# Adding the memory sums' epsilon during eviction, with new cuts around the weighing and a new order of banks in the tail

## The chip, the cores and the metric

The kernel runs on one core of one Trainium2 chip. The metric is device microseconds (us) of a whole execution. Most executions of one kernel agree within 0.3%. A profiled execution is one execution; its span is from first to last instruction. All comparisons below are between runs in the fast state (granted TensorE clock 1.0).

## The reference, cut to what matters

The program computes `x + A(layernorm(x)) + B(x)`. B is a gated-MLP-like block over the sequence and is not touched. A is attention in four segments of 512 rows with 32 heads, plus a linear "memory" that is carried from segment to segment:

```python
for s in range(N):                                   # 4 segments
    logits = einsum('bhqd,bhkd->bhqk', qs, ks) * scale + mask
    p = softmax(logits); a_dot = einsum('bhqk,bhkd->bhqd', p, vs)
    pq  = phi(qs)
    num = einsum('bhld,bhde->bhle', pq, M)
    den = einsum('bhld,bhd->bhl', pq, z)[..., None] + 1e-06      # the epsilon in question
    a_mem = num / den
    outs.append(g * a_mem + (1.0 - g) * a_dot)
    M, z = M + ..., z + ...
return o @ wo
```

Of the kernel before, what the change touches and what calls it, by code (L numbers as in the profile page):

```python
# [7 lines left out]
ALU = mybir.AluOpType  # L8
# [378 lines left out]
class _Kernel:  # L387
# [33 lines left out]
    def alloc(self):  # L421
        k = _Walk(self.mem, 0, self.G_AT)

        def one(name, shape, dtype):
            t, (r,) = k.take(name, shape, dtype)
            setattr(self, name, t)
            setattr(self, "R_" + name, r)

        one("ident", [P, P], BF16)
        self.brow1, self.R_brow1 = k.take("brow1", [P, 32], BF16, 5)  # L430
        self.brow2, self.R_brow2 = k.take("brow2", [P, 32], BF16, 5)
        one("bcol", [P, 2, 32], BF16)
        one("b1c", [P, N_FCH], F32)
        one("b2c", [P, N_TCH], F32)
        one("beta", [P, N_HEAD], BF16)
        one("gcol", [P, N_HEAD], F32)
        one("gate", [P, N_GRP, 2, 4], F32)
        one("eps8", [P, 2, 4], F32)
        self.ln_st, self.R_st = k.take("ln_st", [P, N_TCH, 12], F32, N_TCH)
        self.ln_mv = k.take("ln_mv", [P, N_TCH, 2], F32)[0]  # L440
        self.ln_rs, self.R_rs = k.take("ln_rs", [P, N_TCH, 2], F32, N_TCH)
        self.R_rs0 = Res("rs0")
        one("expo", [P, N_TCH], F32)
        self.ln_sm = k.take("ln_sm", [P, N_TCH, 1], F32)[0]
        self.srec, self.R_srec = k.take("srec", [P, 2, 32], F32, 2)
        self.R_out = [Res(f"out{c}") for c in range(N_TCH)]

        e = _Walk(self.mem, self.G_AT, self.B_AT)
        one_e = e.take("junk", [P, D_MODEL], BF16)
        self.junk, (self.R_junk,) = one_e  # L450
        self.warm, (self.R_warm,) = e.take("warm", [P, 512], BF16)
        e.at = self.G_AT + 14336
        self.w1early, self.R_w1e = e.take("w1early", [P, N_TCH, 512], BF16, N_TCH)
        e.at = self.G_AT + 3 * 14336
        self.xin, self.R_xin = e.take("xin", [P, N_TCH, D_MODEL], BF16, N_TCH)

        b = _Walk(self.mem, self.B_AT + 6400, self.SB_END - self.SB_BASE)
        self.h = [[None, None], [None, None]]
        R = [[None, None], [None, None]]
        for k2 in range(2):  # L460
            both, res = b.take(f"h{k2}", [P, 2, 8, 512], F16, 1)
            self.mem.live.pop()
            for d in range(2):
                self.h[k2][d] = both[:, d]
                R[k2][d] = [Res(f"h{k2}{d}_{i}") for i in range(8)]
                lo = self.SB_BASE + b.at - 16384 + 8192 * d
                self.mem.live.append((lo, lo + 8192, R[k2][d]))
            setattr(self, f"h_{k2}", both)
        self.R_h = R
        self.hT, self.R_hT = [], []  # L470
        for i in (0, 1, 3):
            t, (r,) = b.take(f"hT{i}", [P, 8, 512], F16)
            self.hT.append(t[:])
            self.R_hT.append([r])
        self.hT.insert(2, self.h[0][1])
        self.R_hT.insert(2, R[0][1])
        self.w1s, self.R_w1s = [], []
        for i in range(2):
            t, (r,) = b.take(f"w1s{i}", [P, N_TCH, 256], BF16)
            self.w1s.append(t)  # L480
            self.R_w1s.append(r)
        self.s1, self.R_s1 = [], []
        for i in range(2):
            t, r = b.take(f"sum1_{i}", [P, 4, 8, P], F16, 4)
            self.s1.append(t)
            self.R_s1.append(r)
        self.tmp, self.R_tmp = [], []
        for i in range(6):
            t, (r,) = b.take(f"part{i}", [P, 512], F32)
            self.tmp.append(t)  # L490
            self.R_tmp.append(r)
# [55 lines left out]
    def gates(self):  # L547

        fw = self.fw
        fw.op("pool", lambda e: e.memset(self.eps8[:, 0, :], 0.0), writes=[self.R_eps8])  # L550
        fw.op("pool", lambda e: e.memset(self.eps8[:, 1, :], MEM_EPS), reads=[self.R_eps8], writes=[self.R_eps8])
        fw.op("act", lambda e: e.activation(self.gcol[:], self.beta[:], ACT.Exp, scale=-1.0),
              reads=[self.R_beta], writes=[self.R_gcol])
        fw.op("dve", lambda e: e.tensor_scalar(self.gcol[:], self.gcol[:], 1.0, None, op0=ALU.add),
              reads=[self.R_gcol], writes=[self.R_gcol])
        fw.op("dve", lambda e: e.reciprocal(self.gcol[:], self.gcol[:]), reads=[self.R_gcol], writes=[self.R_gcol])
        gv = self.gcol[:].rearrange("p (g r) -> p g r", r=4)
        fw.op("dve", lambda e: e.tensor_scalar(self.gate[:, :, 0, :], gv, -1.0, 1.0, op0=ALU.mult, op1=ALU.add),
              reads=[self.R_gcol], writes=[self.R_gate])
        fw.op("dve", lambda e: e.tensor_copy(self.gate[:, :, 1, :], gv),  # L560
              reads=[self.R_gcol, self.R_gate], writes=[self.R_gate])
# [580 lines left out]
    def before_attention(self, p):  # L1142
# [42 lines left out]
        elif p == 3:  # L1185
            self.pT = take("pT", [P, 2, 4, PT_COLS], BF16)[0]
            base = self.mem.live.pop()
            self.R_pu = [[Res(f"pu{b}{k}", dict(base[2][0].r)) for k in range(4)] for b in range(2)]
            self.R_pd = [[Res(f"pd{b}{k}", dict(base[2][0].r)) for k in range(4)] for b in range(2)]
            self.mem.live.append((base[0], base[1], [r for rows in self.R_pu + self.R_pd for r in rows]))  # L1190
            self.xnT[1], self.R_xnT[1] = take("xnT1", [P, N_DCH, SEG_L], BF16, 4)
            w = _Walk(self.mem, self.B_AT, self.B_AT + self.S2_AT)
            self.MZ32, self.R_MZ32 = w.take("MZ32", [P, N_GRP, GW], F32, N_GRP)
            self.MZbf, self.R_MZbf = w.take("MZbf", [P, N_GRP, GW], BF16, N_GRP)
            self.diag, (self.R_diag,) = w.take("diag", [P, 4, VW], F32)
            self.oT, self.R_oT = [], []
            for k in range(2):
                t, r = w.take(f"oT{k}", [P, N_GRP, SEG_L], BF16, N_GRP)
                self.oT.append(t)
                self.R_oT.append(r)  # L1200
            w = _Walk(self.mem, self.B_AT + 88320, self.B_AT + 96512)
            self.fin, self.R_fin = [], []
            for k in range(4):
                t, r = w.take(f"fin{k}", [P, D_MODEL], BF16, 2)
                self.fin.append(t)
                self.R_fin.append(r)
            fw.op("dve", lambda e: e.memset(self.diag[:], 0.0), writes=[self.R_diag])
            for r in range(4):
                fw.op("dve", lambda e: e.memset(self.diag[32 * r:32 * r + 32, r, :], 1.0),
                      reads=[self.R_diag], writes=[self.R_diag])  # L1210
# [161 lines left out]
    def weigh(self, u, part):  # L1372
# [37 lines left out]
        else:  # L1410
            q0 = (0, 2, 3)[part]
            dst = self.ost[o][:].rearrange("p (q a) x -> p q (a x)", q=4)[:, q0:q0 + n, 0:GW]
            src = self.ps[:, b, 0:n * GW].rearrange("p (q y) -> p q y", y=GW)
        fw.op("dve", lambda e: e.tensor_copy(dst, src), reads=[self.R_bank[b]], writes=[self.R_ost[o][part]])  # L1414
        if upd:
            src = self.ps[:, b, 2 * GW:3 * GW]
            m32, mbf = self.MZ32[:, g, :], self.MZbf[:, g, :]
# [9 lines left out]
    def combine(self, u):  # L1427
# [22 lines left out]
        def scales():  # L1450
            sums = ost[:, :, D_HEAD].rearrange("p (q a) -> p q a", q=4)
            rv = rec.rearrange("p (q a) -> p q a", q=4)
            e8 = self.eps8[:].rearrange("p k r -> p (k r)")[:, None, :].to_broadcast([P, 4, 8])
            g8 = self.gate[:, g, :, :].rearrange("p k r -> p (k r)")[:, None, :].to_broadcast([P, 4, 8])
            fw.op("dve", lambda e: e.tensor_tensor(rv, sums, e8, op=ALU.add), reads=R_ost + [self.R_eps8], writes=[R_rec])
            fw.op("dve", lambda e: e.reciprocal(rec, rec), reads=[R_rec], writes=[R_rec])
            fw.op("dve", lambda e: e.tensor_tensor(rv, rv, g8, op=ALU.mult), reads=[R_rec, self.R_gate], writes=[R_rec])

        def products():
# [58 lines left out]
    def attention(self):  # L1518
# [11 lines left out]
        for u in range(N_UNIT):  # L1530
# [13 lines left out]
            if u in self.XN_AT[::4]:  # L1544
                self.xn_load(xn)
                self.xn_load(xn + 1)
            if u < 10 or u >= 14 and total <= 26:
                cuts = self.cut(total, (0, 4, 2, 4, 1, 13, 8) if even else (7, 3, 2, 4, 1, 15))
            else:
                cuts = self.cut(total, (0, 4, 2, 2, 2, 14, 8) if even else (7, 3, 2, 2, 2, 16))  # L1550
# [46 lines left out]
    def tail(self):  # L1597
# [5 lines left out]
        fw.wait_outputs(3)  # L1603

        def product(n, j0, j1, cols=((0, 512),)):
            i, h, b = n // 2, n % 2, (0, 1, 2, 3, 6, 7, 5, 4)[n]
            for p, (c0, c1) in enumerate(cols):
                with fw.group(reads=self.R_wo[j0:j1] + self.R_oT[s % 3][j0:j1], writes=[self.R_bank[b]]):
                    for jc in range(j0, j1):
# [24 lines left out]
        product(4, 0, 7)  # L1634
        self.o_transpose(u, 4)
        product(3, 6, 7)
        product(5, 0, 7)
        for n in range(6):
            product(n, 7, 8)
        product(6, 0, 8)  # L1640
        product(7, 0, 8, ((0, 256), (256, 384), (384, 512)))

# [27 lines left out]
```

## The kernel before: what the change touches

Attention is cut into 32 units u (4 segments of 8 groups of 4 heads). In unit u, TensorE does the logits of u in steps, and the *weighing* (softmax weights and memory times values) of unit u-1 in three parts; dense 512-column matmuls (the projections `wq`, `wv`, `wo`) fill the gaps. `cuts` says how many of them stand between those steps. Between the logits and the weighing, ScalarE takes the exponential and the pool engine (POOL, GpSimd) masks the diagonal blocks in place.

```python
# --- attention(), unit u: where the dense matmuls stand
if u < 10 or u >= 14 and total <= 26:
    cuts = self.cut(total, (0, 4, 2, 4, 1, 13, 8) if even else (7, 3, 2, 4, 1, 15))
else: ...
self.dense(cuts[0]);  self.logits(u, 0)
self.dense(cuts[1]);  self.weigh(u - 1, 0)
self.dense(cuts[2]);  self.weigh(u - 1, 1)
self.dense(cuts[3]);  self.weigh(u - 1, 2)
#   ... VectorE's work is queued: scales, phi_q(u), products, add (then the transposing DMA oT <- o_s)
self.dense(cuts[4]);  self.logits(u, 1)
if even:
    self.dense(cuts[5]); self.logits(u, 2)      # third logits: blocks of u AND of u + 1
self.dense(rest)
# --- weigh(): a part leaves PSUM (12 x 33 columns = 396, or 264)
fw.op("dve", lambda e: e.tensor_copy(dst, src), reads=[self.R_bank[b]], writes=[self.R_ost[o][part]])
# --- combine(), segments 1 to 3
def scales():
    fw.op("dve", lambda e: e.tensor_tensor(rv, sums, e8, op=ALU.add), ...)      # + epsilon, 128 x 32
    fw.op("dve", lambda e: e.reciprocal(rec, rec), ...)
    fw.op("dve", lambda e: e.tensor_tensor(rv, rv, g8, op=ALU.mult), ...)
def products():   # prod <- ost * srec, 128 x 1024, both inputs in SBUF
def add():        # o_s <- prod + prod
# --- tail(): the last output product, after the last unit
i, h, b = n // 2, n % 2, (0, 1, 2, 3, 6, 7, 5, 4)[n]         # the bank of product n
product(0, 0, 6); product(1, 0, 6); self.weigh(u, 0); self.weigh(u, 1); product(2, 0, 6); self.weigh(u, 2)
for step in self.combine(u): step()
product(3, 0, 6)
for n in range(3): product(n, 6, 7)             # needs unit 30's transposed result (jc = 6)
product(4, 0, 7); self.o_transpose(u, 4); product(3, 6, 7)
product(5, 0, 7)
for n in range(6): product(n, 7, 8)
...
```

An even unit's third logits belong half to the next unit. So the weighing of an odd unit's result happens in an even unit and needs that odd unit's first mask.

## Time and profile before

| | before |
|---|---|
| median of 3 runs | 654.29 us (654.28 to 654.56) |
| median of 6 runs (these 3 and 3 more), beside the kernel after | 654.42 us (654.12 to 654.98) |
| span of the profiled run | 652.2 us |

From the page of the kernel before, the line of busy times (us, share of the span, instructions) and the first line of the chain that ended last:

```profile
PE 646.7 (99%) x4611; PEld 303.1 (46%) x4611; DVE 439.9 (67%) x829; ACT 281.5 (43%) x305; POOL 154.9 (24%) x181
...
PE 90%; DVE 4%; DMA 2%; ACT 1%; POOL 1%; issue 1%; DVEq 0%
```

TensorE is the limit. The Trainium skill ("Perfetto Trace Analysis", § Identifying the Most-Contended Engine) warns that matmul busy time is a poor measure, because matmuls are pipelined; this case agrees, since the page says 98 or 99% for every fast run here, and 99% for the one that saves 3.3 us. What was used instead is the distance between the starts of neighbouring matmuls in the trace, less the length of the matmul (0.213 us for 512 columns) and the fixed step at a change of matmul kind. What remains is called a *stall* below.

Groups of instructions of the kernel before (out<-in, shapes, count | busy us, mean ns | idle before it), VectorE and then POOL:

```profile
L1460 DVE TENSOR_TENSOR prod<-ost,srec 128x1024 bf16<-128x1024 bf16 x24 | 35.1, 1461 | 0.0
L1414 DVE CAST ost<-ps_all 128x396 bf16<-128x396 f32 x48 | 26.4, 564 | 10.6 <-PE ps_all L199 10.2
...
L1455 DVE TENSOR_TENSOR srec<-ost,eps 128x32 f32<-128x32 bf16 x24 | 4.8, 202 | 0.3
...
L1367 POOL TENSOR_SCALAR_AFFINE_SELECT pT<-pT 128x512 bf16<-128x512 bf16 x128 | 106.3, 847 | 160.9 <-ACT pT L1363 160.9
```

The product `prod` and the mask `pT<-pT` have means (1461 and 847 ns) that hide two populations. The timeline of the kernel before shows them (columns: start us, duration us, engine, line, operation). Unit 24 first (VectorE, the pool engine, TensorE), then unit 26 (the same order):

```profile
575.27 0.69 DVE L1229 SCALAR_TENSOR_TENSOR pqT<-qT,mtmp 128x512 bf16<-128x512 bf16 x1
575.88 1.68 DVE L1460 TENSOR_TENSOR prod<-ost,srec 128x1024 bf16<-128x1024 bf16 x1
...
575.84 0.63 POOL L1367 TENSOR_SCALAR_AFFINE_SELECT pT<-pT 128x512 bf16<-128x512 bf16 x1 [2.78 <-ACT pT L1363]
...
576.25 0.82 PE L199 MATMUL ps_all<-wo,oT 128*128 128x512 bf16 x3
576.91 0.26 PE L199 MATMUL ps_all<-vA,pT 128*128 128x33 bf16 x4
...
590.06 1.22 DVE L1460 TENSOR_TENSOR prod<-ost,srec 128x1024 bf16<-128x1024 bf16 x1
...
590.43 1.34 POOL L1367 TENSOR_SCALAR_AFFINE_SELECT pT<-pT 128x512 bf16<-128x512 bf16 x1 [2.55 <-ACT pT L1363]
...
591.92 0.25 PE L199 MATMUL ps_all<-vA,pT 128*128 128x33 bf16 x4 [0.19 <-POOL pT L1367]
```

In unit 24 the mask starts 0.04 us before the product: the mask takes 0.63 us and the product 1.68. In unit 26 the product starts first: the product takes 1.22 us and the mask 1.34. Whoever comes first runs undisturbed (the mask in 0.63, the product in 1.22 us). TensorE's weighing (`vA,pT`) waits for the mask, so the second order is the expensive one: in unit 24 the weighing starts 0.22 us after the start of the 512-column matmul before it, in unit 26 it starts 0.57 us after, so it stalls for 0.35 us.

The tail of the kernel before on TensorE and on the queue of SyncE, which issues the transposing DMA:

```profile
631.74 1.90 PE L199 MATMUL ps_all<-wo,oT 128*128 128x512 bf16 x8
633.89 2.75 PE L199 MATMUL ps_all<-wo,oT 128*128 128x512 bf16 x12 [0.24 <-ACT pT L1363]
...
637.49 1.19 SPq L221 DMA_TRANSPOSE oT<-o_s  x1
```

The first product of the tail waits for the last exponential (bank 0 is still being read). Unit 30's result is issued for its transpose at 637.49 us, and the product that needs it loses 0.16 us.

### The profile page before, as it was taken

What the parts mean: (1) busy time and instruction counts of PE and PEld (TensorE: products, weight loads), DVE (VectorE), ACT (ScalarE), POOL (GpSimd) and SP (SyncE); (2) the same over time, 40 slices, a digit from 0 to 9 for tenths busy, and PEclk for the clock granted to TensorE, in tenths of its full rate; (3) what the DMA queues carried; (4) which work ended last, traced back from release to release, by engine and by line L of the source; (5) the groups of instructions that cost most, each with busy time, mean ns of one, the idle gap of its engine ahead of it and who ended that gap; (6) DMA issues with size and microseconds to landing.
All of it is one profiled execution on the core that took longest, in us unless ns stands there. A gap on an engine that the chain in (4) does not pass through costs nothing.

```text
span 652.2 us, 11204 instructions
## 1 busy us (share of the span) xinstructions
PE 646.7 (99%) x4611; PEld 303.1 (46%) x4611; DVE 439.9 (67%) x829; ACT 281.5 (43%) x305; POOL 154.9 (24%) x181
## 2 busy tenths in 40 slices
PE   9999999999999999999999999999999999999998
PEld 3444444444444444444444444444545444454444
DVE  6975775665655673745637325767898988887895
ACT  7542232232210000111101047778767788888760
POOL 2500000000011220120201203434333445544450
PEclk9999999999999999999999999999999999999999
DMA  8804242242498937629263956979644576355424
GB/s 300 217 0 130 65 116 79 65 124 70 129 265 216 231 96 210 171 87 258 66 193 116 257 136 156 190 182 227 124 120 109 152 164 144 90 115 123 114 81 138
DMA packets 190123, 95.00 MB, mean 146 GB/s; under 512 B 108664, under 2 KB 176248, under 8 KB 190072
## 3 DMA queue, kind: packets, MB, share of 16 engines
q1 hardware_dynamic: 189928, 94.25, 56.9%
q8 instruction: 36, 0.59, 0.4%
q14 instruction: 15, 0.12, 0.1%
q10 hardware_dynamic: 144, 0.03, 0.0%
HBM read 69.23 MB, written 11.53 MB: 124 GB/s over the span
## 4 chain that ended last, share of the span: by engine, by line
PE 90%; DVE 4%; DMA 2%; ACT 1%; POOL 1%; issue 1%; DVEq 0%
PE ps_all L199 90%; ACT pT L1363 1%; DMA w2s<-in_B_w_dram 1%; POOL pT L1367 1%; DVE fin L1617 1%; DVE ln_st L590 1%; DVE sum L651 0%; DVE prod L1460 0%; DMA xin<-in_A_x_dram 0%; DVE h L630 0%; POOL ln_rs L614 0%; DVE mtmp L1229 0%; DVE mtmp L1227 0%; DVE ost L1414 0%; DVE part L692 0%
## 5 line engine op out<-in xcount | busy, mean ns | idle before, releaser
L1363 ACT ACTIVATE pT<-ps_all 128x2048 bf16<-128x2048 f32 x80 | 150.2, 1877 | 47.2 <-PE ps_all L199 46.8
L1367 POOL TENSOR_SCALAR_AFFINE_SELECT pT<-pT 128x512 bf16<-128x512 bf16 x128 | 106.3, 847 | 160.9 <-ACT pT L1363 160.9
L692 DVE TENSOR_TENSOR part<-ps_all,part 128x512 f32<-128x512 f32 x84 | 57.7, 690 | 108.9 <-PE ps_all L199 88.2
L1078 POOL TENSOR_TENSOR part<-part,stg 128x512 f32<-128x512 f32 x24 | 33.0, 1402 | 285.0 <-DVE part L692 268.1
L749 ACT ACTIVATE g<-part,b1c 128x512 f16<-128x512 f32 x36 | 26.0, 722 | 99.0 <-DVE part L692 99.0
L199 PE MATMUL ps_all<-wv,xnT 128*128 128x512 bf16 x256 | 68.2, 380 | 0.2
L199 PE MATMUL ps_all<-xnT,wq 128*128 128x512 bf16 x256 | 65.6, 380 | 0.0
L199 PE MATMUL ps_all<-wo,oT 128*128 128x512 bf16 (+2 forms) x272 | 64.3, 367 | 0.2 <-ACT pT L1363 0.2
L1414 DVE CAST ost<-ps_all 128x396 bf16<-128x396 f32 (+2 forms) x96 | 44.3, 473 | 27.3 <-PE ps_all L199 26.6
L697 ACT ACTIVATE part<-ps_all 128x512 f32<-128x512 f32 x24 | 14.0, 596 | 101.4 <-PE ps_all L199 67.1
L199 PEld LDWEIGHTS ps_all<-vA,pT 128*128 128x128 bf16 x1280 | 45.5, 96 | 21.5 <-DVE ost L1414 3.3
L199 PE MATMUL ps_all<-g,sum 128*128 128x512 f16 x224 | 51.0, 379 | 0.0
L199 PE MATMUL ps_all<-g,w2s 128*128 128x512 f16 x224 | 51.0, 379 | 0.0
L199 PE MATMUL ps_all<-gT,sum 128*128 128x512 f16 x224 | 50.3, 379 | 0.1
L199 PE MATMUL ps_all<-vA,pT 128*128 128x33 bf16 x1280 | 48.5, 178 | 0.7 <-POOL pT L1367 0.6
L199 PE MATMUL ps_all<-h,sum 128*128 128x512 f16 x192 | 45.2, 379 | 0.0
L199 PE MATMUL ps_all<-h,w1s 128*128 128x512 f16 x192 | 44.9, 379 | 0.0
L199 PE MATMUL ps_all<-hT,sum 128*128 128x512 f16 x192 | 43.6, 379 | 0.0
L199 PEld LDWEIGHTS ps_all<-wo,oT 128*128 128x128 bf16 x272 | 23.8, 97 | 27.1 <-issue 4.9
L1460 DVE TENSOR_TENSOR prod<-ost,srec 128x1024 bf16<-128x1024 bf16 x24 | 35.1, 1461 | 0.0
L199 PEld LDWEIGHTS ps_all<-gT,sum 128*128 128x128 f16 x224 | 21.8, 98 | 26.8 <-DVE gT L666 0.6
L199 PEld LDWEIGHTS ps_all<-g,w2s 128*128 128x128 bf16 x224 | 21.9, 98 | 26.4
(118 smaller groups left out, 862.2 us busy)
## 6 DMA issues: line engine op xcount, KB each, us to landing
w2s<-in_B_w_dram SPq DMA_DIRECT2D x8, 1792.0 KB, 9.5
w1s<-in_B_w_dram SPq DMA_DIRECT2D x12, 1024.0 KB, 5.6
wq<-in_A_wq_dram SPq DMA_DIRECT2D x32, 256.0 KB, 3.4
xs<-in_A_x_dram SPq DMA_DIRECT2D x24, 256.0 KB, 3.4
stg<-in_A_x_dram SPq DMA_DIRECT2D x16, 256.0 KB, 2.8
out_dram<-stg SPq DMA_DIRECT2D x16, 256.0 KB, 3.8
wk<-in_A_wk_dram SPq DMA_DIRECT2D x16, 256.0 KB, 3.4
fin<-out_dram SPq DMA_DIRECT2D x16, 256.0 KB, 3.3
```

What stands on the lines that cost most here:

```text
L199: ins = self.nc.tensor.matmul(*args, **kwargs)
L590: fw.op("dve", lambda e: e.bn_stats(st[:, 6 * h:6 * h + 6], src[:, 512 * h:512 * h + 512]), reads=[self.R_xin[c]], writes=[R])
L692: self.fw.op("dve", lambda e: e.tensor_tensor(self.tmp[dst][:], self.bank(b), self.tmp[src][:], op=ALU.add), reads=[self.R_bank[b], self.R ...
L697: self.fw.op("act", lambda e: e.activation(self.tmp[dst][:], self.bank(b), ACT.Copy), reads=[self.R_bank[b]], writes=[self.R_tmp[dst]])
L749: self.fw.op("act", lambda e: e.activation(self.gB[f % 2][half][:, f // 2, :], src, ACT.Gelu_apprx_tanh, bias=self.b1c[:, f:f + 1], scale= ...
L1078: fw.op("pool", lambda e: e.tensor_tensor(self.tmp[t][:], self.tmp[t][:], self.stg[k][:, 512 * half:512 * half + 512], op=ALU.add), reads= ...
L1363: fw.op("act", lambda e: e.activation(dst, src, ACT.Exp, scale=SCALE), reads=self.R_bank[0:4], writes=[R[v % 2][kb] for v, kb, _ in blocks ...
L1367: fw.op("pool", lambda e: e.affine_select(d, d, pattern=[[0, 4], [1, P]], compare_op=ALU.is_ge, fill=0.0, base=0, channel_multiplier=-1), ...
L1414: fw.op("dve", lambda e: e.tensor_copy(dst, src), reads=[self.R_bank[b]], writes=[self.R_ost[o][part]])
L1460: fw.op("dve", lambda e: e.tensor_tensor(self.prod[:], ost[:, :, 0:D_HEAD], rec.unsqueeze(2).to_broadcast([P, 32, D_HEAD]), op=ALU.mult), ...
L1617: fw.op("dve", lambda e: e.tensor_tensor(dst, self.ps[:, b, c0:c1], dst.bitcast(F16), op=ALU.add), reads=[self.R_bank[b], R], writes=[R])
```

## The change

The intent: take a 0.2 us operation out of VectorE's chain in each of 24 units (the eviction, which must run anyway, adds a constant tile that is zero but for the memory sums' columns), give the weighing of the later even units one more matmul of cover, and let the tail begin in banks that the last exponential does not hold.

```diff
@@ weigh()
-        fw.op("dve", lambda e: e.tensor_copy(dst, src), reads=[self.R_bank[b]], writes=[self.R_ost[o][part]])
+        if s:
+            e0 = GW * (part % 2)
+            eps = self.eps[:].rearrange("p k r x -> p (k r x)")[:, e0:e0 + n * GW]
+            fw.op("dve", lambda e: e.tensor_tensor(dst, src, eps, op=ALU.add), reads=[self.R_bank[b], self.R_eps],
+                  writes=[self.R_ost[o][part]])
+        else:
+            fw.op("dve", lambda e: e.tensor_copy(dst, src), reads=[self.R_bank[b]], writes=[self.R_ost[o][part]])
@@ combine(), scales()
-            fw.op("dve", lambda e: e.tensor_tensor(rv, sums, e8, op=ALU.add), reads=R_ost + [self.R_eps8], writes=[R_rec])
-            fw.op("dve", lambda e: e.reciprocal(rec, rec), reads=[R_rec], writes=[R_rec])
+            fw.op("dve", lambda e: e.reciprocal(rv, sums), reads=R_ost, writes=[R_rec])
@@ attention()
-            if u < 10 or u >= 14 and total <= 26:
+            if u >= 18 and even:
+                cuts = self.cut(total, (0, 4, 1, 4, 0, 9, 6))
+            elif u < 10 or u >= 14 and total <= 26:
@@ tail()
-            i, h, b = n // 2, n % 2, (0, 1, 2, 3, 6, 7, 5, 4)[n]
+            i, h, b = n // 2, n % 2, (6 + self.turn, 0, 1, 2, 3, 7 - self.turn, 5, 4)[n]
-        product(5, 0, 7)
-        for n in range(6):
+        product(5, 0, 5)
+        for n in range(5):
             product(n, 7, 8)
+        product(5, 5, 8)
# cut: two small pool-engine memsets of the old epsilon tile go, three VectorE memsets of the new one come
```

More of the change, by code (lines that the diff above doesn't have):

```diff
@@ L437, in alloc @@
         one("gate", [P, N_GRP, 2, 4], F32)
-        one("eps8", [P, 2, 4], F32)
         self.ln_st, self.R_st = k.take("ln_st", [P, N_TCH, 12], F32, N_TCH)
@@ L549, in gates @@
         fw = self.fw
-        fw.op("pool", lambda e: e.memset(self.eps8[:, 0, :], 0.0), writes=[self.R_eps8])
-        fw.op("pool", lambda e: e.memset(self.eps8[:, 1, :], MEM_EPS), reads=[self.R_eps8], writes=[self.R_eps8])
         fw.op("act", lambda e: e.activation(self.gcol[:], self.beta[:], ACT.Exp, scale=-1.0),
@@ L1195, in before_attention @@
             self.diag, (self.R_diag,) = w.take("diag", [P, 4, VW], F32)
+            self.eps, (self.R_eps,) = w.take("eps", [P, 4, 4, VW], F32)
+            fw.op("dve", lambda e: e.memset(self.eps[:], 0.0), writes=[self.R_eps])
+            for k in (1, 3):
+                fw.op("dve", lambda e: e.memset(self.eps[:, k, :, D_HEAD:], MEM_EPS), reads=[self.R_eps], writes=[self.R_eps])
             self.oT, self.R_oT = [], []
@@ L1452, in scales @@
             rv = rec.rearrange("p (q a) -> p q a", q=4)
-            e8 = self.eps8[:].rearrange("p k r -> p (k r)")[:, None, :].to_broadcast([P, 4, 8])
             g8 = self.gate[:, g, :, :].rearrange("p k r -> p (k r)")[:, None, :].to_broadcast([P, 4, 8])
-            fw.op("dve", lambda e: e.tensor_tensor(rv, sums, e8, op=ALU.add), reads=R_ost + [self.R_eps8], writes=[R_rec])
-            fw.op("dve", lambda e: e.reciprocal(rec, rec), reads=[R_rec], writes=[R_rec])
+            fw.op("dve", lambda e: e.reciprocal(rv, sums), reads=R_ost, writes=[R_rec])
             fw.op("dve", lambda e: e.tensor_tensor(rv, rv, g8, op=ALU.mult), reads=[R_rec, self.R_gate], writes=[R_rec])
```

## The prediction

> **What bounds it.** The page gives TensorE 99% busy; 512-column matmuls start every 0.213 us, and the chain of waits is 90% matmul. TensorE's start-to-start gaps in the timeline, less the matmuls' own length and the fixed steps around the logits, leave about 5.6 us of real stalls after 375 us. So VectorE's 67% (82% in the last quarter) costs only where it makes TensorE wait.
>
> **Costs.**
> - The epsilon operation: 24 x 0.202 us (groups of instructions), 0.23 us start to start, so 5.5 us of VectorE time goes. It stands before reciprocal, scale and products, which come 0.23 us earlier.
> - The eviction becomes a tensor-tensor add. 132 columns cost 280 ns as add and 284 as copy; 512 columns with add 690 against 688. So 396 columns stay near 0.57 us: free.
> - The cuts of even units from 18 on: of 24 dense matmuls old 0,3,1,4,0,10,6, new 0,4,1,4,0,9,6. One matmul (0.213 us) moves ahead of the weighing.
> - Tail: the first product no longer waits for the last exponential.
>
> **On the critical path (timeline).**
> 1. Units 26, 28, 30: the weighing stalls 0.35, 0.42, 0.35 us for the mask of the pool engine, which starts 0.37 us after VectorE's product (1.22 us) and takes 1.34 us instead of 0.64. Product 0.23 earlier plus one matmul of cover: stalls go, -1.1 us.
> 2. Units 16 to 24: here the mask starts 0.036 us BEFORE the product: mask 0.64 us, product 1.67 us. With the product 0.2 us earlier the order flips; the mask then ends at product start + 1.71 us, 0.9 us later than now. Less the moved matmul this makes new stalls of about 0.26, 0.05, 0.39, 0.24, 0.39 us, against old stalls there (0.21, 0.21, 0.10, 0, 0.09, behind late VectorE work) that vanish: +0.7 us. The Trainium skill, "SBUF — State Buffer", § Who interferes with whom, says that issue order decides who blocks; the durations here agree.
> 3. Even units 18 to 30: between the second and third logits stand 9 matmuls, not 10. The third logits start 0.267 us after the exponential ends; where nine stand (odd to even units, from 20 on) they start 0.145 after it and lose 0.09. Seven times: +0.6 us.
> 4. Tail: the 0.41 us wait for the last exponential goes; the 0.16 us wait for unit 30's transpose goes too, as product and mask flip there; VectorE's last evictions start two matmuls earlier. -0.7 us.
>
> Sum: -0.5 us.
>
> **Prediction:** 653.6 us, 8 in 10 between 652.3 and 654.6. Faster by over 2%: 0.005; within 2%: 0.99; slower by over 2%: 0.005.
>
> **What would show it.** The 24 epsilon operations gone; evictions 0.56-0.58 us; VectorE busy about 435 us. Masks before units 16 to 24: first 1.5 us, products 1.22 (now 0.64 and 1.67). Weighing waits at 26, 28, 30 gone, new ones at 20, 22, 24. Third logits 0.145 us after the exponential. In the tail no gap at the first product; last eviction about 0.2 us after the last matmul (now 0.46).
>
> **What would make it wrong.** If the flip of step 2 does not come, or new evictions shift it, 0.7 us more is gained (652.9). If an eviction with a second operand is slower by 0.1 us, 72 of them shift VectorE back and the stalls stay. If the tail is bound by the transpose's landing, 0.4 us less is gained.

## The result and the profile after

| | before | after |
|---|---|---|
| median of 6 runs | 654.42 us (654.12 to 654.98) | 653.0 us (652.66 to 653.41) |
| ratio of the fast runs, 95% interval | | 0.9978 (0.9965 to 0.9991) |
| span of the profiled run | 652.2 us | 651.3 us |

Ratios, here and below, are the mean time of one kernel's fast runs over that of the other's fast runs of the same rounds, so not quite the ratio of the medians. The change saves 1.4 us in the medians (0.9 us in the two profiled spans). The predicted 653.6 us and its range hold.

The page and the groups of the kernel after; VectorE's busy time fell by 6.2 us, TensorE's stays at 99%:

```profile
PE 645.6 (99%) x4611; PEld 303.2 (47%) x4611; DVE 433.7 (67%) x808; ACT 281.3 (43%) x305; POOL 153.0 (23%) x179
...
PE 94%; DVE 2%; DMA 1%; ACT 1%; POOL 1%; issue 0%; DVEq 0%
```

```profile
L1465 DVE TENSOR_TENSOR prod<-ost,srec 128x1024 bf16<-128x1024 bf16 x24 | 29.5, 1228 | 0.0
L1418 DVE TENSOR_TENSOR ost<-ps_all,eps 128x396 bf16<-128x396 f32 x48 | 26.6, 566 | 12.2 <-PE ps_all L199 11.6
...
L1368 POOL TENSOR_SCALAR_AFFINE_SELECT pT<-pT 128x512 bf16<-128x512 bf16 x128 | 104.5, 834 | 161.9 <-ACT pT L1364 161.7
```

The epsilon operation (4.8 us) is gone, and the eviction with an addition costs 566 ns where the copy cost 564. The Trainium skill ("VectorE: DVE Perf Modes", § Why PSUM operands drop a tier) says that an fp32 PSUM operand leaves a VectorE operation in its slowest mode in any case; these two durations agree. That this is the reason why the addition is free here is the page's account; no run tests it. The product's mean fell from 1461 to 1228 ns: 23 of the 24 products now take about 1.22 us, as one that comes first does. Units 24 and 26 in the timeline of the kernel after, VectorE and pool engine, and then TensorE in both:

```profile
575.84 1.22 DVE L1465 TENSOR_TENSOR prod<-ost,srec 128x1024 bf16<-128x1024 bf16 x1
...
576.04 1.51 POOL L1368 TENSOR_SCALAR_AFFINE_SELECT pT<-pT 128x512 bf16<-128x512 bf16 x1 [2.78 <-ACT pT L1364]
...
590.29 1.22 DVE L1465 TENSOR_TENSOR prod<-ost,srec 128x1024 bf16<-128x1024 bf16 x1
590.90 1.10 POOL L1368 TENSOR_SCALAR_AFFINE_SELECT pT<-pT 128x512 bf16<-128x512 bf16 x1 [2.55 <-ACT pT L1364]
```

```profile
576.45 1.04 PE L199 MATMUL ps_all<-wo,oT 128*128 128x512 bf16 x4
577.70 0.25 PE L199 MATMUL ps_all<-vA,pT 128*128 128x33 bf16 x4 [0.21 <-POOL pT L1368]
...
591.38 1.04 PE L199 MATMUL ps_all<-wv,xnT 128*128 128x512 bf16 x4
592.25 0.26 PE L199 MATMUL ps_all<-vA,pT 128*128 128x33 bf16 x4
```

In unit 24 the order has flipped: product 1.22 us, mask 1.51 us in place of 0.63, and the weighing waits for it (the bracket is the idle time that the profile sees; against the usual distance between the starts the stall is 0.37 us). In unit 26 the mask starts later after the product and ends 0.49 us after the product's end; with one more matmul ahead of it, the weighing no longer waits.

The stalls of the weighing in the two traces from unit 15 on, in us (the unit is that in which the weighing stands):

| unit | 15 | 16 | 18 | 20 | 22 | 24 | 26 | 28 | 30 | sum |
|---|---|---|---|---|---|---|---|---|---|---|
| before | 0.18 | 0.21 | 0.22 | 0.10 | 0 | 0.09 | 0.35 | 0.43 | 0.35 | 1.93 |
| after | 0.05 | 0.25 | 0.04 | 0.38 | 0.23 | 0.37 | 0 | 0 | 0 | 1.32 |

The tail of the kernel after, TensorE and the DMA issue, and then the chain of waits over 634 to 641 us:

```profile
631.74 3.83 PE L199 MATMUL ps_all<-wo,oT 128*128 128x512 bf16 x17
...
637.95 1.46 PE L199 MATMUL ps_all<-wo,oT 128*128 128x512 bf16 x6
639.94 0.39 PE L199 MATMUL ps_all<-wo,oT 128*128 128x512 bf16 x1 [0.53 <-DMA oT<-o_s]
...
635.64 2.03 SPq L221 DMA_TRANSPOSE oT<-o_s  x1
```

```profile
635.64 4.25 DMA oT<-o_s
639.90 0.05 issue
639.94 1.25 PE ps_all L199 x5
```

The wait for the last exponential is gone (0.41 us). But the wait for unit 30's transpose has grown from 0.16 to 0.70 us of stall, although the transpose was issued 1.85 us earlier: it took 4.25 us to land, where before it took 2.93. From unit 31's first logits to the end of the last eviction both kernels take 21.12 us: up to there the tail gained nothing.

### The profile page after: what moved, and what is told of

Its sections match the earlier page's. It is cut to its first block, busy times and chain, and to the rows that moved or that the text cites. A ratio compares the mean times of both kernels' runs of the same rounds, so it can differ in the third digit from the quotient of the medians.

```text
span 651.3 us, 11181 instructions
## 1 busy us (share of the span) xinstructions
PE 645.6 (99%) x4611; PEld 303.2 (47%) x4611; DVE 433.7 (67%) x808; ACT 281.3 (43%) x305; POOL 153.0 (23%) x179
## 4 chain that ended last, share of the span: by engine, by line
PE 94%; DVE 2%; DMA 1%; ACT 1%; POOL 1%; issue 0%; DVEq 0%
PE ps_all L199 94%; ACT pT L1364 1%; DMA oT<-o_s 1%; DVE ln_st L587 1%; POOL pT L1368 0%; DMA xin<-in_A_x_dram 0%; DVE h L627 0%; POOL ln_rs L611 0%; DVE mtmp L1230 0%; DVE mtmp L1228 0%; DVE prod L1465 0%; DVE pqT L1230 0%; DVE fin L1307 0%; DVE ln_mv L590 0%; DVE kT L1262 0%
## 5 line engine op out<-in xcount | busy, mean ns | idle before, releaser
L1368 POOL TENSOR_SCALAR_AFFINE_SELECT pT<-pT 128x512 bf16<-128x512 bf16 x128 | 104.5, 834 | 161.9 <-ACT pT L1364 161.7
L1418 DVE TENSOR_TENSOR ost<-ps_all,eps 128x396 bf16<-128x396 f32 (+1 forms) x72 | 37.0, 522 | 24.3 <-PE ps_all L199 23.7
L199 PEld LDWEIGHTS ps_all<-g,sum 128*128 128x128 f16 x224 | 21.9, 98 | 26.4 <-DVE part L689 0.2
```

The lines of the kernel that those rows point to most:

```text
L199: ins = self.nc.tensor.matmul(*args, **kwargs)
L1368: fw.op("pool", lambda e: e.affine_select(d, d, pattern=[[0, 4], [1, P]], compare_op=ALU.is_ge, fill=0.0, base=0, channel_multiplier=-1), ...
L1418: fw.op("dve", lambda e: e.tensor_tensor(dst, src, eps, op=ALU.add), reads=[self.R_bank[b], self.R_eps], writes=[self.R_ost[o][part]])
```

## The experiments

Twelve runs were made, all correct (e6 and e6b are one kernel, run twice). Those of one call share the runs of the kernel before: 654.5 us in the first call (e1, e2, e3, e8), 654.37 in the second (e4, e5, e6, e10), 654.38 in the third (e6b, e12, e13, e14). The first 387 us, which no edit touches in substance, vary by up to 0.7 us between the profiled runs, so where tenths matter the text compares stalls, not spans.

### Each part of the change alone: e1, e2, e3

The three parts were put into the kernel before one at a time. Each run below is the change's diff reduced to that part.

**e1_eps_alone**

```diff
  # weigh() and scales() as in the kernel after; cuts and tail as in the kernel before
-            if u >= 18 and even:
-                cuts = self.cut(total, (0, 4, 1, 4, 0, 9, 6))
-            elif u < 10 or ...
+            if u < 10 or ...
```

> Only the epsilon moves into the evictions; cuts and tail as before. Order theory (the shorter chain makes the product start before the mask instead of 0.036 us after it, in units 16 to 24): weighing stalls of about 0.26, 0.26, 0.60, 0.45, 0.60 us at units 16, 18, 20, 22, 24, 0.12 to 0.20 at 26, 28, 30; the wait of 0.41 us for the last exponential stays; 0.3 to 0.7 us SLOWER than before. Rival (less VectorE work is simply a gain, and the new stalls of the whole change come from its cuts): no new stalls, 26 to 30 shrink by 0.2 each, about 0.7 us faster.

Measured: 655.23 us (654.68 to 655.29), ratio 1.0009 (0.9996 to 1.0021): the interval holds 1, and the profiled span is 0.7 us longer than that of before. Faster VectorE work alone does not help. The stalls at units 16 to 24 are 0.25, 0.26, 0.59, 0.44 and 0.59 us (sum 2.13, before 0.62), those at 26 to 30 only fall to 0.12, 0.19 and 0.12. So the removed operation alone makes the order flip at all of these units, and without the extra matmul of cover the long mask is fully paid for. In the tail the stall for the transpose is 0.50 us (before 0.16): it lands 4.46 us after its issue (before 2.93), so the shorter VectorE chain alone brings the late landing that the kernel after shows.

**e2_cuts_alone**

```diff
+            if u >= 18 and even:
+                cuts = self.cut(total, (0, 4, 1, 4, 0, 9, 6))
-            if u < 10 or ...
+            elif u < 10 or ...            # all else as in the kernel before
```

> Only the cuts of the even units from 18 on; epsilon operation and tail as before. Order theory: the mask still starts first at 18 to 24 (0.64 us, product 1.67), no stalls of 0.25 or more there; stalls at 26, 28, 30 fall by one matmul from 0.35, 0.42, 0.35 to 0.14, 0.21, 0.14; about 0.6 us faster. Third logits about 0.056 us after the exponential without a stall, as in the whole change. Rival (the cuts make the new stalls): 0.2 to 0.4 us at 20, 22, 24 appear here, no gain.

Measured: 654.25 us (654.11 to 655.08), ratio 0.9999 (0.9986 to 1.0011). At 26, 28 and 30 the stalls fall to 0.14, 0.21 and 0.14 us, as one matmul of cover (0.213 us) should do. But at 20 and 24 they grow from 0.10 and 0.09 to 0.48 us. The cause is in the timelines of this run, TensorE and then VectorE:

```profile
578.46 0.81 PE L199 MATMUL ps_all<-wv,xnT 128*128 128x512 bf16 x3
...
576.00 1.68 DVE L1460 TENSOR_TENSOR prod<-ost,srec 128x1024 bf16<-128x1024 bf16 x1
...
578.37 0.68 DVE L1306 TENSOR_TENSOR fin<-ps_all,fin 128x512 bf16<-128x512 f32 x1
578.97 0.55 DVE L1414 CAST ost<-ps_all 128x396 bf16<-128x396 f32 x1
```

The moved matmul ends an output product before the weighing, so VectorE's eviction of that product (`fin`) now stands ahead of the weighing's first eviction. With the slow 1.68 us product (mask first) VectorE is late, the first cast comes at 578.97 us, and the weighing's third part waits for its bank. In the kernel after the product is fast and that does not happen. The expected 0.6 us did not come. The rival named stalls at 20 to 24 too, but as the work of the cuts alone; in the kernel after, with the same cuts, this wait for a bank is not there. So the cuts and the removed operation need each other.

**e3_tail_alone**

```diff
  # only the two edits of tail(), all else as in the kernel before (cut: the new order of products 0 to 5, as in the change)
-            i, h, b = n // 2, n % 2, (0, 1, 2, 3, 6, 7, 5, 4)[n]
+            i, h, b = n // 2, n % 2, (6 + self.turn, 0, 1, 2, 3, 7 - self.turn, 5, 4)[n]
```

> Only the banks and the order of the tail. Theory (the tail's next wait is the landing of unit 30's transpose, whatever comes before it): the wait of 0.41 us for the last exponential goes, and the wait for the transpose grows from 0.16 to about 0.57 us; TensorE ends at the same time, the last eviction 0.2 to 0.3 us earlier; 0.2 to 0.3 us faster. Rival (in the whole change it was the earlier VectorE chain that brought the transpose into a worse place among the transfers): transpose wait stays near 0.16, 0.6 us faster.

Measured: 653.72 us (653.46 to 654.83), ratio 0.999 (0.9977 to 1.0002). In the trace the 0.41 us wait for the exponential is gone and the transpose's stall stays at 0.15 us (landing in 2.91 us); from unit 31's logits to the last eviction it takes 20.58 us in place of 21.12, so 0.54 us. From there to the end of the span it takes another 0.26 us less (1.95 in place of 2.21). So the rival held, and not the theory: alone, the tail's edit is worth what was predicted for it (0.7 us) or a little more; in the kernel after the first part of its gain is eaten.

The three differences in the medians (+0.7, -0.25, -0.8 us) sum to about -0.3 us; together the parts gave -1.4. The parts are not additive, because the cover pays for the flip.

### Is it the order, or the shorter chain? e8

```diff
+        one("zero8", [P, 2, 4], F32)                 # zeros (cut: the pool-engine memset that writes them)
-            fw.op("dve", lambda e: e.reciprocal(rv, sums), reads=R_ost, writes=[R_rec])
+            fw.op("dve", lambda e: e.tensor_tensor(rv, sums, z8, op=ALU.add), reads=R_ost + [self.R_zero8], writes=[R_rec])
+            fw.op("dve", lambda e: e.reciprocal(rec, rec), reads=[R_rec], writes=[R_rec])
```

The kernel after, with an addition of zeros where the epsilon's stood: the result is the same, the delay is back.

> The whole change, and an addition of zero put where the epsilon operation stood (same shape, same place), so the VectorE chain is as long as before while the evictions still carry the epsilon. Order theory: the mask starts about 0.04 us before the product again in units 16 to 24 (mask 0.64, product 1.67 us), the stalls of 0.25, 0.38, 0.23, 0.37 at the first weighing go, the old small ones (0.2, 0.1, 0.1) come back, 26, 28, 30 stall 0.14, 0.21, 0.14; time within 0.3 us of the whole change. Rival (the evictions' second operand, read from SBUF, or the cuts delay the mask): the stalls of 0.23 to 0.38 stay and the time is 0.3 to 0.6 us above the whole change.

Measured: 653.53 us (653.14 to 653.68), ratio 0.9983 (0.997 to 0.9997). The two lines of unit 24, VectorE and pool engine:

```profile
576.40 1.67 DVE L1469 TENSOR_TENSOR prod<-ost,srec 128x1024 bf16<-128x1024 bf16 x1
...
576.36 2.20 POOL L1370 TENSOR_SCALAR_AFFINE_SELECT pT<-pT 128x512 bf16<-128x512 bf16 x2 [2.78 <-ACT pT L1366]
```

The mask again starts 0.04 us before the product (x2 merges two masks; the first takes 0.63 us) and the product is slow again. So 0.23 us of VectorE time, and nothing else of the change, decides the order at units 16 to 24. Its stalls (0.21, 0, 0.48, 0, 0.48, 0.14, 0.21, 0.14 us at the even units from 16) are those of e2. Two things were not as expected: 0.48 us stands at units 20 and 24 where the old 0.1 was expected, and the time is 0.5 us above the kernel after, not within 0.3. The time alone would have spoken for the rival; the starts and lengths in the trace decide for the order. The stall for the transpose is 0.22 us (it lands in 3.06 us), and there is none for the exponential.

### The transpose in the tail: e4, e10, e14

**e4_tail_cover**: the kernel after, with six matmuls that need no fresh result moved ahead of the ones that wait.

```diff
         product(3, 0, 6)
+        product(4, 0, 6)
         for n in range(3):
             product(n, 6, 7)
-        product(4, 0, 7)
+        product(4, 6, 7)
```

> The whole change, with the six matmuls of the tail's fifth product that need no late transpose put ahead of the first ones that need unit 30's transpose (1.28 us of cover). Theory (the tail waits for the landing of that transpose, 0.70 us in the whole change, with nothing else behind it): that wait goes, TensorE and the span end 0.6 to 0.7 us earlier than the whole change, about 2.0 us under before. Rival (the next thing in line is as late, for instance unit 31's combined output or the VectorE's last evictions): the span gains under 0.2 us and a new wait stands before the last transposes.

Measured: 652.36 us (652.09 to 652.75), ratio 0.9969 (0.9957 to 0.9982), profiled span 650.9. The transpose is even later here (issued 635.94, landed 4.64 us later), and no stall for it is left. From unit 31's logits to the last matmul it takes 19.87 us, in the kernel after 20.57. So the 0.7 us that the tail lost in the kernel after was this one wait, and six matmuls (1.3 us) cover it.

Why does the transpose land late? Against e3 and before, the kernel after issues it earlier and meets other transfers. Two instruction fetches stand near it in the trace: one of 16 KB and one of 8 KB. In before, e2, e3 and e8 the 8 KB fetch is at 607 us, in after, e1, e4 and e10 at 637; the late landings are those of the second group. (e5, described below, has the 8 KB fetch at 637 us and lands early, in 2.85 us, but it issues later than all, at 639.35 us.)

**e10_pad**: 21 idle VectorE writes before the attention, so that VectorE's instruction count is that of the kernel before.

```diff
+        self.pad, self.R_pad = k.take("pad", [P, 24], F32, 24)
         elif p == 2:                                # (lines between the two places are cut)
+            for n in range(21):
+                fw.op("dve", lambda e: e.memset(self.pad[:, n:n + 1], 0.0), writes=[self.R_pad[n]])
```

> The whole change, with 21 tiny memsets of one column before the attention, where VectorE idles, so that its program has as many instructions as before. Theory (with fewer VectorE instructions the fetch of its next instructions, 8 KB, moves from about 607 us to 636.5 us and meets unit 30's transpose, which lands 4.25 us after its issue instead of 2.9): the fetch is back near 607, the transpose lands in 2.9 to 3.1 us, the tail's wait falls from 0.70 to at most 0.2 us, 0.5 us faster. Rival (it is TensorE's own 16 KB fetch near 636 or the other transfers that the earlier transpose meets): it still lands in about 4.2 us and the wait stays above 0.5.

Measured: 653.66 us (653.16 to 653.79), ratio 0.9987 (0.9975 to 1.0). The 8 KB fetch stayed at 636.8 us, so this run did not set up what it was to test; the transpose landed in 4.87 us. It shows only that the fetch does not follow VectorE's instruction count.

**e14_idle_memset**: a single idle write on the pool engine instead.

```diff
+        one("zero8", [P, 2, 4], F32)
+        fw.op("pool", lambda e: e.memset(self.zero8[:], 0.0), writes=[self.R_zero8])     # in gates(); nothing reads it
```

> The kernel after with a single idle write of eight zeros on the pool engine at the start, which nothing reads. It tests why unit 30's transposed result lands late. Theory of the instruction fetch: the 8 KB fetch that stands at 636.5 us in the kernels with the late landing, and at 607 us in those with the early one, belongs to the pool engine's instructions, of which the kernel before has two more; one more is enough to bring it back to 607 us (the run with the idle addition had one too). Then the transpose lands in about 3.0 us in place of 4.25, TensorE's wait of 0.70 us for it falls to about 0.2 or less, and the time is about 652.5 us. Rivals: the fetch goes back to 607 us and the transpose is still late (then the fetch is not what delays it, and the earlier issue is), or nothing moves at all (then the fetch is not the pool engine's, and the question stays open): 653.0 us in both.

Measured: 652.9 us (652.37 to 653.54), ratio 0.9977 (0.9964 to 0.9989). The 8 KB fetch went back, to 606.8 us: it follows the pool engine's instructions. And the transpose is still late:

```profile
635.96 2.84 SPq L221 DMA_TRANSPOSE oT<-o_s  x1
```

It landed in 4.35 us, and the stall is 0.80 us. So the 8 KB fetch is not the cause: that theory fell. What is left is the 16 KB fetch, or the other transfers under way. In this run the 16 KB fetch starts at 636.2 us and takes 1.59 us, in the middle of the issue. There are thirteen fast traces. In the eight where the transpose of unit 30 is issued before the 16 KB fetch has ended (after, e1, e4, e6b, e10, e12, e13, e14) it lands in 4.25 to 4.87 us; in the five that issue it after that fetch (before, e2, e3, e5, e8) it lands in 2.85 to 3.06. Over the 273 transposes of `o_s` after 455 us whose landing the thirteen traces hold, the median landing is 3.9 us with a 16 KB fetch in the 2.4 us after the issue or still under way at it (98 of them), and 2.42 without (175). That is an association, and not a strict one: 28 of the 98 landed within 2.9 us, 17 of the 175 took longer, and of those issued before 455 us, 58 of 83 without such a fetch took over 2.9 us too. SyncE's issues point the same way: the load just ahead of the transpose takes 0.92 us in the kernel before, where the fetch stands beside it, and 0.43 in the kernel after, where the fetch stands beside the transpose's own issue (2.03 us in place of 1.19). No run moved the 16 KB fetch alone. Why the one delays the other stays open.

### Can the masks be made short again? e5

```diff
                 self.side.append(steps.pop(0))          # scales
+                if u > N_GRP:
+                    self.side.append(steps.pop(0))      # products, ahead of phi_q
             if N_GRP <= u:
                 self.side.append(lambda u=u: self.phi_q(u))
```

> The whole change, with VectorE's product of a unit put ahead of the two feature operations of the next query, so that it starts about 0.95 us earlier. Order theory: in odd units the product is over about when the masks begin (first mask 0.64 to 0.95 us instead of 1.5, it may now meet the feature operations), the first-weighing stalls at 16, 20, 22, 24 (0.25, 0.38, 0.23, 0.37) go; 1.0 to 1.2 us faster than the whole change, about 2.5 us under before. Rival (those stalls come from the length of the VectorE's queue[...]): stalls stay within 0.1 us of what they are.

Measured: 655.44 us (655.11 to 655.87), ratio 1.0017 (1.0003 to 1.0031): slower. The masks did get short (the first takes 0.70 us), but the weighing now waits for something else. TensorE in unit 20 of this run, and VectorE:

```profile
548.60 0.27 PE L199 MATMUL ps_all<-vA,pT 128*128 128x33 bf16 x4 [0.49 <-DVE pqT L1230]
...
546.78 0.72 DVE L1228 TENSOR_SCALAR mtmp<-etmp 128x512 bf16<-128x512 bf16 x1
547.54 1.00 DVE L1230 SCALAR_TENSOR_TENSOR pqT<-qT,mtmp 128x512 bf16<-128x512 bf16 x1
```

The feature `pqT` is read by that same weighing, and it now stands behind the product. The two feature operations, which now run beside the masks, also take 0.72 and 1.00 us, where they took 0.28 and 0.69 in the kernel before. Stalls at units 16 to 24: 0.54, 0.32, 0.66, 0.51, 0.67 us. The design of this experiment missed a dependency; the order of VectorE's work was right as it was.

### What are the 0.09 us before an even unit's first logits? e6, e6b

The prediction charged 0.6 us for the third logits, because where nine matmuls stand between two logits the later one starts 0.145 us after the exponential and stalls by 0.09. The kernel after has nine matmuls there and no stall: the third logits start 0.055 us after the exponential (before 0.267). So the 0.145 belongs to something else. The first logits of units 20 to 30 need two things on TensorE's queue, one after the other: the exponential (their bank) and a DMA (the keys, long landed).

```diff
         reads = [R for v in units for R in (self.R_kT[v % 3], self.R_qT[v % 3])]
+        if step == 1 and u % 2 and N_UNIT // 2 <= u + 1 < N_UNIT:
+            reads.append(self.R_kT[(u + 1) % 3])        # wait for the next unit's keys here already
```

> The whole change, with TensorE told of the landing of the next unit's keys one logits group earlier, so that the first logits of even units from 16 on wait for one semaphore, not for two one after the other. Theory for the failed third step of the prediction (the 0.09 us at those logits is the second wait instruction, not the distance of nine matmuls): from unit 20 on the first logits start 0.056 us after the exponential instead of 0.145, stalls of 0.09 at units 20, 22, 24, 26, 28, 30 go; 0.5 us faster than the whole change. Rival (nine matmuls are too few for the exponential): 0.145 and 0.09 stay, no gain.

Measured: 653.18 us median, ratio of the fast runs 0.9981 (0.9967 to 0.9995). One of its five runs, the profiled one, took 1315.89 us, twice the others (its 512-column matmuls start 0.44 us apart in place of 0.213, at a granted clock of 0.986); nothing is concluded from its trace. The kernel ran once more.

> The kernel after, with one wait moved: the odd unit's second logits already wait for the keys of the next even unit, so that the first logits of the even units 18 to 30 meet only one wait, the one on the exponential. (A repeat of the run before it, whose profile fell on an execution at half speed.) Theory of two waits: the stall of 0.09 us before these logits is the price of two waits one after the other on TensorE's queue; then the first logits start about 0.06 us after the exponential ends, as the third logits do, in place of 0.145, six to seven stalls of 0.09 us go, and the time is about 652.5 us. Rival, the distance: nine matmuls between two logits are simply too few to cover the exponential; then the 0.145 us and the stalls stay, and the time is that of the kernel after, 653.0 us.

Measured: 653.18 us (652.64 to 653.75), ratio 0.9979 (0.9965 to 0.9993), so no faster than the kernel after. The theory of the two waits is confirmed and the gain is not. Unit 26 in the kernel before (ScalarE's exponential, then TensorE) and in this run:

```profile
588.48 1.88 ACT L1363 ACTIVATE pT<-ps_all 128x2048 bf16<-128x2048 f32 x1 [0.79 <-PE ps_all L199]
...
590.50 0.40 PE L199 MATMUL ps_all<-qT,kT 32*128 32x512 bf16 x4
```

```profile
588.88 1.88 ACT L1366 ACTIVATE pT<-ps_all 128x2048 bf16<-128x2048 f32 x1 [0.79 <-PE ps_all L199]
...
590.81 0.39 PE L199 MATMUL ps_all<-qT,kT 32*128 32x512 bf16 x4
```

The logits start 0.14 us after the exponential's end (588.48 + 1.88 = 590.36) in the first, and 0.05 us in the second; in all six units it is 0.145 against 0.055 in exact numbers, and all six stalls of 0.09 us (0.54 us in all) are gone. But the gain comes back as waiting at the next place. At units 22, 26 and 30 the 512-column matmul right after the logits waits for an eviction that stands behind the exponential on ScalarE and comes no earlier: in unit 26 of this run `vA` ends at 591.24 us and that matmul starts at 591.30, and its stall grew from 0.07 to 0.16 us. At units 20 and 24 the earlier logits only made the weighing wait longer for its mask (0.47 us in place of 0.37), and at 28 a new stall of 0.06 us stands there. From unit 20 to unit 31, 0.03 of the 0.54 us is kept. In the tail the stall for the transpose was 1.06 us in place of 0.70. At the eight odd units whose second logits now carry the wait for the keys, it costs nothing: their distance from the logits before them is that of the kernel after, within 0.002 us. (The recorded distance from the matmul before them grows from 0.312 to 0.369 us, but only because the record of one matmul is missing in this trace, as in all but two of them; e12, without the early wait, shows 0.369 too.) So the second wait cost 0.09 us where TensorE was waiting for the exponential, and nothing where both waits had long been met.

### The better version: e12, e13

If the new stalls at 16 to 24 are the long mask alone, two more matmuls of cover must remove them with the mask left as it is.

```diff
  # e12: the kernel after, e4's edit, and
-            if u >= 18 and even:
-                cuts = self.cut(total, (0, 4, 1, 4, 0, 9, 6))
+            if u >= 16 and even:
+                cuts = self.cut(total, (0, 6, 1, 2, 0, 9, 6))
  # e13: e12 and e6's edit
```

> The kernel after with the tail's cover (six matmuls of the fourth product block moved ahead of the transposed result) and, in the even units from 16 on, two more matmuls ahead of the weighing (six in place of four before its first part, two in place of four between its second and third). Theory of the masks: what is left of the new stalls at units 16, 20, 22 and 24 (0.25, 0.38, 0.23, 0.37 us) is the long mask of 1.5 us alone, and 0.43 us of cover takes all of it away; the masks stay as long as they are. Then the stalls at these units are under 0.05 us each and the time is 1.0 to 1.2 us below that of the tail's cover alone, about 651.3 us. Rival: the third part of the weighing, now two matmuls closer to the second, waits for its bank as it did where the cut was moved alone; then stalls of about 0.4 us come back before the third part and the time is 652.2 us or more.

Measured: 651.06 us (650.99 to 651.29), ratio 0.9949 (0.9936 to 0.9961), profiled span 649.2. Pool engine and TensorE in unit 24 of this run:

```profile
575.06 1.51 POOL L1368 TENSOR_SCALAR_AFFINE_SELECT pT<-pT 128x512 bf16<-128x512 bf16 x1 [2.77 <-ACT pT L1364]
...
576.34 0.59 PE L199 MATMUL ps_all<-wv,xnT 128*128 128x512 bf16 x2
576.77 0.26 PE L199 MATMUL ps_all<-vA,pT 128*128 128x33 bf16 x4
```

The mask still takes 1.51 us, and the weighing no longer waits: no stall above 0.03 us at a weighing is left from unit 16 on, and no third part waits for its bank. Against e4 the median is 1.3 us lower, which is the sum of the stalls that went (0.25 + 0.04 + 0.38 + 0.23 + 0.37 = 1.27 us).

> The run before this one and the early wait for the keys together. If both theories hold, their gains add, since they lie at different places of each unit: stalls under 0.05 us both at the weighing and at the first logits of the even units, about 650.8 us. If the early wait is worth nothing, the time is that of the run before this one.

Measured: 651.0 us (650.82 to 651.16), ratio 0.9947 (0.9935 to 0.996). The early wait is worth 0.06 us here, within the noise. In the traces, from unit 20 to unit 31, 0.21 of the 0.54 us is kept against e12: with the waits for the masks gone, units 20, 24 and 28 keep some of it (0.05 to 0.09 us each), while units 22, 26 and 30 still lose it to ScalarE's eviction. The expected 650.8 us overlooked that wait.

So e12 is the version to keep: 3.3 us below the kernel before, where the change alone saved 1.4.

## Why the prediction was right or wrong

The time (653.6 predicted, 653.0 measured, inside the range) was right, and its first two steps were right in mechanism and size. Two of its four steps were wrong, by -0.6 and +0.7 us (measured less predicted, up to the last eviction). Those two errors cancel, so that the sum came out so close is in part luck. (The prediction's 653.6 us is also 0.7 us below the 654.29 us measured before it, although its steps sum to -0.5.)

| step of the prediction | predicted | measured in the traces |
|---|---|---|
| 1. stalls at 26, 28, 30 go | -1.1 us | -1.13 us |
| 2. flip of mask and product at 16 to 24 (and the late work at 15 and 18 goes) | +0.7 us | +0.52 us, units 15 to 24 |
| 3. third logits, seven times | +0.6 us | 0 |
| 4. tail | -0.7 us | 0.0 us (-0.41 exponential, +0.54 transpose, -0.13 last eviction), and -0.25 us behind the last eviction, which no step named |
| sum | -0.5 us | -0.6 us, with the last -0.85 us |

- **The costs were right.** The eviction stayed free (564 to 566 ns), the epsilon operation gave back 4.8 us of VectorE's time, and VectorE's busy time came to 433.7 us (about 435 predicted). As the prediction said, none of that counted by itself; e1 shows that it can even cost.
- **Step 1 was right.** e1 and e2 show that each half (product earlier, one matmul of cover) leaves 0.12 to 0.21 us, and the two together nothing.
- **Step 2 was right.** The predicted new stalls were 0.26, 0.05, 0.39, 0.24 and 0.39 us; measured 0.25, 0.04, 0.38, 0.23 and 0.37. e8 flips the order back with one idle operation. The size of the step differs from +0.7 mainly because the old stalls that went were somewhat larger (0.80 us with unit 15, not 0.6). The rule that made this computable is the one cited from the Trainium skill.
- **Step 3 was wrong.** The sentence that failed is "where nine stand ... they start 0.145 after it and lose 0.09": the number was read off logits that differ from the third logits in more than the distance. They carry a second wait, and e6b shows that this wait makes the difference (0.145 to 0.055 us with the distance unchanged). The third logits, with nine matmuls before them, start 0.055 us after the exponential and lose nothing.
- **Step 4 was wrong in one term.** "The 0.16 us wait for unit 30's transpose goes too" assumed that an earlier issue means an earlier landing. It was issued 1.85 us earlier and landed only 0.53 us earlier (637.49 + 2.93 against 635.64 + 4.25), while the matmuls that need it came earlier by more. The prediction had named this as its risk ("if the tail is bound by the transpose's landing, 0.4 us less is gained"). e4 shows that this one wait held the tail; e1 and e8 show that the late landing comes with the shorter VectorE chain (4.46 us with it, 3.06 with the idle addition), and why it lands late stays open. The last eviction ends 0.55 us after the start of the last matmul, before 0.68: 0.13 us where about 0.26 was expected.

With the quarter microsecond behind the last eviction (2.21 us before, 1.96 after; 1.95 to 1.97 in every run with the new tail, 2.21 or 2.22 in those with the old one), the table accounts for about -0.85 of the -0.9 us between the profiled spans. The medians of the times differ by 1.4 us. Of the rest, 0.33 us lies outside the spans: the time is longer than the span by 2.02 to 2.14 us in every fast run of before, e2, e3 and e10, and by 1.68 to 1.84 in every one of the others, e1 included. No step predicted this part, and what makes it is not shown (e10 differs from the kernel after only by 21 idle writes on VectorE, and has the 2.1 us again). The remaining 0.15 to 0.2 us is within the spread of single runs.

## What to carry to other kernels

When an operation leaves the chain of an engine that is not the bottleneck, ask which two operations of different engines, of those that slow each other when they overlap, change their order; here 0.23 us decided whether a mask took 0.63 or 1.51 us, and the bottleneck paid for it until it had enough work of its own in front of that wait. Cover at the bottleneck (more independent matmuls ahead of the wait) was worth more than speed off it: e12 took all of those stalls away with the masks as slow as before. A duration read at one place carries over to another only if the two places have the same waits. A stall that is taken away may come back at the next wait behind it, as in e6b, so follow the gain to the end of the unit. And an issue that comes earlier may meet other traffic and land hardly earlier.

## What the Trainium skill lacked or had wrong

- "SBUF — State Buffer", § Who interferes with whom, says that issue order decides who blocks and that the later one is blocked fully; the runs agree on the order (mask first by 0.04 us: 0.63 and 1.68 us; product first by 0.2 us: 1.22 and 1.51 us). Read literally, the loser would need its whole own time after the winner's end. Here it needed less: the blocked mask ended 0.49 us after the product's end in units 24 and 26 alike (577.06 to 577.55, 591.51 to 592.00), although alone it takes 0.63, and the blocked product of unit 24 before ended 1.09 us after the mask's end (576.47 to 577.56), although alone it takes 1.22. Recorded starts tell the order only to some 0.02 us: beside a mask recorded 0.03 us ahead the product took 1.68 us, beside one recorded 0.01 us ahead (product at 567.7 us of the kernel after) it took 1.22 and the mask 1.73.
- No page that was looked up gives the price of two waits one after the other on TensorE's queue: 0.145 us from the exponential's end to the logits in place of 0.055 (e6b), and no delay at the eight places where both waits had long been met.
- "DMA: Bandwidth & Descriptors" fits a transfer as about 2.0 us plus bytes over 436 GB/s (for another kind of DMA queue); as an estimate that is 2.3 us for these 128 KB transposes. Those after 455 us without a 16 KB instruction fetch near their issue agree (median 2.42 us). It does not say what an instruction fetch does to a transfer near it: with one near their issue they took 3.9 us in the median and up to 4.87, an association only.
- "Perfetto Trace Analysis" recommends the busy share of weight loads, beside the share of peak arithmetic (MFU), in place of matmul busy time. In these kernels the first reads 46 to 47% whether 3.3 us of stalls are left or not, since a weight load takes 0.096 us of each 0.213 us matmul; the starts of the matmuls had to be read.
